# Scores formed one item ahead, a fourth buffer for the decayed r, and routing steps behind the mask products

## Chip, cores and metric

One core of a Trainium2 chip. The metric is device time in microseconds (us) of one execution; a profiled execution is shown beside the plain ones. The engines are TensorE (PE; its weight loads are listed as PEld), VectorE (DVE), ScalarE (ACT), GpSimd (POOL) and SyncE (SP), which issues most DMAs. Each engine works through its own instructions in order; semaphores hold an instruction until what it needs has been done elsewhere.

## What is computed

An RWKV-5 attention over 4 batches of 8 heads, 768 tokens and 48 dimensions, followed by a mixture of 8 experts in which each token goes to one expert; a token whose local gate is 0.5 or more takes the expert of the token before it.

```python
def _attn_ref(r, k, v, w, u):
    for t in range(S):
        kt, vt, rt = (k[:, :, t], v[:, :, t], r[:, :, t])
        cur = np.einsum('bhd,bhe->bhde', u[None] * kt, vt)
        y[:, :, t] = np.einsum('bhd,bhde->bhe', rt, state + cur)
        state = w[None, :, :, None] * state + np.einsum('bhd,bhe->bhde', kt, vt)

def _moe_ref(x, w_gate, w_local, w1, w2):
    logits = np.einsum('bsd,de->bse', x, w_gate)
    local_gate = 1.0 / (1.0 + np.exp(-np.einsum('bsd,de->bse', x, w_local).squeeze(-1)))
    for b in range(B):
        prev_e = -1
        for s in range(S):
            fresh_e = int(np.argmax(logits[b, s]))
            e = fresh_e if s == 0 or local_gate[b, s] < 0.5 else (prev_e if prev_e >= 0 else fresh_e)
            prev_e = e
            ...
            h = np.maximum(x[b, s] @ w1[e], 0.0)
            out[b, s] = p[e] * (h @ w2[e])
```

Here p is the softmax of the token's logits.

## The kernel before, in words

The kernel has two stages. The attention stage (`Attention.run`) takes the first 120 us or so, the experts (`Experts.run`) the rest. The change lies in the attention stage and in the routing steps (`Router`) that are woven into it.

**Items.** The attention is cut into M = 16 items, n = 0 to 15: 4 batches by 4 pairs of heads (HP = 4). An item is one batch and two heads, all 768 tokens, in six chunks of 128 tokens (NCH). Within a chunk the sum over earlier tokens is formed as a masked product of scores with v; what came before the chunk enters through a state S.

**The steps of one item**, with the engine that carries them and the line that the profile shows:
- `load` (SP, L199, L203, L204): three DMAs, r and k transposed (rk), k and v by token (kv), v transposed (vT). rk and vT have 4 buffers in turn, kv has 5. `load(n + 3)` stands at the head of iteration n.
- `scale` (POOL): ke (L217, k times powers of the decay up to the chunk's end), rw (L234, r times powers of the decay, in `decayed`) and pd (L221, r times k), each in two halves. ke and pd have two buffers, rw three. `scale(n + 1)` is issued in iteration n. From item 3 on the order is ke, rw, pd; for items 0 to 2 rw is formed on VectorE, in `keys`.
- `keys` (VectorE, L241): kw, k divided by powers of the decay; two buffers.
- `added` (TensorE, L253): 20 products of ke with v into T, a part of the PSUM tile mp.
- `states` (VectorE, L259): one scan over T that gives S for all chunks.
- `scores` (TensorE, L288, 24 products a call, two calls g = 0 and 1): rw with kw into one of the two PSUM tiles of `pairs`, which `banks` hands out in turn. A call returns the mask product (VectorE, L290), which multiplies the tile with the mask `kept` into am. The name `keep` stands for the second call's mask product, issued later.
- `own` (TensorE, L269, 8 products, then VectorE, L273): u times r times k, summed over the dimensions and laid out into the PSUM tile y; VectorE multiplies it with vT. There is one y tile. This is called the vT product below.
- `inside` (TensorE, L297, 24 products): adds am times v to y.
- `before` (TensorE, L310, 20 products, then ACT, L314): adds S times rw to y; ACT copies y to xT.
- `turn` (TensorE, L323, 6 transposes, then ACT, L325): turns xT to rows x; after the fourth pair of heads of a batch, a DMA on ACT's queue writes x to DRAM.
- `logits` (TensorE, L336, and ACT, L337), once a batch, and `token_logits` (TensorE, L342, and ACT, L343).

**The order of a common iteration n.** The program is written out by hand. TensorE has, in this order, turn(n-2), added(n), inside(n-1), before(n-1), scores(n) twice, own(n). VectorE has kw(n), S(n), the first mask product of n, the vT product of n, the second mask product of n. Where n is a multiple of 4, the second mask product stands before the vT product, and logits follow.

**Routing.** The first two batches (group 0, g = 8 in the code) are routed while the attention of the last two runs, one step an iteration from n = 9 on: `experts_of` (VectorE, L665 to L672), `keys` and `runs` (a transpose on TensorE, L679, then a scan on VectorE, L684), `turn_runs` (a transpose on TensorE, L689, and a copy on ACT to rn, L690), `last` (TensorE, L696), `one_hot` (VectorE, L702 to L709), `counts` (two products on TensorE, L716 and L717), `ranks` (ACT, L723, and VectorE, L724 to L735), `slots` and `columns`, `numbers`, `places` (VectorE, L783, twice), `summed` (TensorE, L790), `copied` (ACT, L796), `head` (a transpose on TensorE, L800, then VectorE, L804 to L821). After `head`, `heads()` issues two gathers of token rows on POOL's queue (L1037), which the first expert turns on TensorE (L1050). Most of these steps use parts of the tile mp, in which T lies too.

Of the kernel before, what the change touches and what calls it, by code (L numbers as in the profile page):

```python
# [11 lines left out]
F32 = mybir.dt.float32  # L12
# [8 lines left out]
P = 128  # L21
# [7 lines left out]
NCH = S // P  # L29
# [32 lines left out]
class Attention:  # L62
# [13 lines left out]
    def __init__(self, tc, st, rk_d, kv_d, vT_d, x_d, w_t, wp_d, kept, ident, lt, mp):  # L76
        self.tc, self.nc = tc, tc.nc
        nc = tc.nc
        self.rk_d, self.kv_d, self.vT_d, self.x_d = rk_d, kv_d, vT_d, x_d
        self.w_t, self.kept, self.ident, self.lt = w_t, kept, ident, lt  # L80

        self.late = st.enter_context(tc.tile_pool(name="late", bufs=1))
        self.wp = self.late.tile([P, H, 32], F32, name="wp")
        self.sel = self.late.tile([P, 2 * (E + 1)], F32, name="sel")
        self.inner = ExitStack()

        def pool(name, bufs, **kw):
            return self.inner.enter_context(tc.tile_pool(name=name, bufs=bufs, **kw))

        once = pool("once", 1)  # L90
        self.two = pool("two", 2)
        self.three = pool("three", 3)
        ps = pool("ps", 1, space=PSUM)

        self.pairs = [ps.tile([P, 2, 512], F32, name=f"pair{i}") for i in range(2)]
        self.py = pool("py", 1, space=PSUM)

        self.T = mp[:, 2 * P + 2:2 * P + 2 + (NCH - 1) * DH].rearrange("p (e c) -> p e c", c=NCH - 1)

        self.inv = pool("pinv", 1, space=PSUM).tile([P, HP, P], F32, name="inv")  # L100


        n = B * HP - 1
        self.rks, self.vTs = [None] * AHEAD, [None] * AHEAD
        for i in range(1, AHEAD + 1):
            self.rks[(n + i) % AHEAD] = once.tile([P, 2, NCH, P], F32, name=f"rk{i}")
        for i in range(1, AHEAD + 1):
            self.vTs[(n + i) % AHEAD] = once.tile([P, 2, C2, P], F32, name=f"vT{i}")
        self.kvs = [once.tile([P, 2 * VB + DP - DH], F32, name=f"kv{i}") for i in range(AHEAD + 1)]
        self.items = [dict() for _ in range(B * HP)]  # L110
        self.xTs, self.xs, self.lTs = {}, {}, {}
        for i in range(AHEAD - 1):
            self.load(i)
        nc.sync.dma_start(out=self.wp, in_=wp_d)


        self.step = once.tile([P, HP, DH, NCH - 1], F32, name="step")
        nc.vector.memset(self.step, 0.0)


        self.tab = tab = once.tile([P, HP, 2, P + 1], F32, name="tab")
        nc.vector.memset(tab[:, 0, :, 0:1], 1.0)
        nc.gpsimd.memset(tab[:, 1:, :, 0:1], 1.0)
        w = once.tile([P, HP, 2], F32, name="w")
        nc.vector.tensor_scalar(w[:, :, 0], w_t[:, :, 0], W_LO, W_HI, Alu.max, Alu.min)
        nc.vector.reciprocal(w[:, :, 1], w[:, :, 0])
        nc.vector.tensor_copy(tab[:, 0, :, 1], w[:, 0])
        nc.gpsimd.tensor_copy(tab[:, 1:, :, 1], w[:, 1:])
        n = 2
        while n <= P:  # L130
            m = min(n - 1, P + 1 - n)
            for engine, t in ((nc.vector, tab[:, :1]), (nc.gpsimd, tab[:, 1:])):
                engine.tensor_mul(t[..., n:n + m], t[..., 1:1 + m], t[..., n - 1:n].to_broadcast([P, t.shape[1], 2, m]))
            n += m

        self.first, self.newton = mp[:, :P + 1], mp[:, P + 1:2 * P + 1]
        nc.scalar.copy(self.first, tab[:, 0, 0])
        self.reciprocals(0)

        self.end = once.tile([P, HP, P + DP], F32, name="end")  # L140
        self.endT = once.tile([P, 2, HP, 2 * DH], F32, name="endT")
        self.align(26)
        self.warm(8)
        self.ends(slice(0, 1))
        self.turn_ends(slice(0, 1))
        self.warm(5)
# [61 lines left out]
    def scale(self, n):  # L208

        nc, t = self.nc, self.items[n]  # L210
        t["ke"] = self.two.tile([P, NCH, 2 * DH], F32, name="ke")
        t["pd"] = self.two.tile([P, NCH, P], F32, name="pd")
        t["rw"] = self.three.tile([P, NCH, P], F32, name="rw")
        hp = t["hp"]

        def ke(p):
            nc.gpsimd.tensor_mul(t["ke"][:, p::2], t["k"][:, p::2], spread(self.endT[:, p, hp], 1, C2))  # L217

        def pd(i):
            z = slice(i * C2, (i + 1) * C2)  # L220
            nc.gpsimd.tensor_mul(t["pd"][:, z], t["rT"][:, z], t["kT"][:, z])  # L221

        def rw(i):
            self.decayed(nc.gpsimd, n, slice(i * C2, (i + 1) * C2))


        for what in (ke, rw, pd) if n > 2 else (pd, ke):
            for i in range(2):
                what(i)

# [114 lines left out]
    def run(self, router, fetch, heads):  # L345
# [11 lines left out]
        for n in range(M + 1):  # L357
# [39 lines left out]
                continue  # L397
            if n < M:
                self.turn(n - 2, pair("tp"))
                if n == 3:  # L400
                    self.added(3)
                    self.reciprocals(3)
                self.keys(n)
                if n > 3:
                    self.added(n)
            if n == g + 2:
                router.keys(0, mp)
            if n == g + 3:
                router.last(0, mp[:, mp_end:])
            if n == g + 4:  # L410
                router.counts(0, [mp, mp[:, E * NC // 2:]])
            if n < M:
                self.states(n)
            if n > HP and n % HP == 1:
# [2 lines left out]
                self.chooser()  # L417
            if n == g + 1:
                router.experts_of(0, (0,))
            if n == g + 2:  # L420
                router.runs(0)
            if n == g + 3:
                router.one_hot(0, (0,))
            if n == g + 4:
                router.ranks(0, (0,))
            if n == g + 5:
# [10 lines left out]
            if n == M:  # L437
                self.turn(M - 2, pair("tp"))
            self.inside(n - 1)
            if n == g + 7:  # L440

                router.summed(0, 0)
                router.copied(0)
            self.before(n - 1)
            if n == 6:
                router.cast()
            if n == M:
                break
            if n == g + 7:
                router.head(pair("tb")[0])  # L450
                heads()
            self.scores(n, 0)()
            keep = self.scores(n, 1)
            if n == g + 1:
                router.experts_of(0, (1,))
            if n == g + 3:
                router.one_hot(0, (1,))
            if n == g + 5:
                router.places(0, 0)
            if n == g + 6:  # L460
                router.places(0, 1)
            if n % HP == 0:

                keep()
                self.own(n)
                self.logits(n // HP - 1, pair("lp")[0])
                if n == g + 4:
                    router.ranks(0, (1,))
            else:
                self.own(n)  # L470
                keep()
            if n == g + 2:
                router.turn_runs(0, mp[:, mp_end:])
        self.inner.close()


# [1228 lines left out]
```

## Time and profile before

| | us |
|---|---|
| plain runs, median of 4 | 388.93 (388.45 to 391.17) |
| profiled execution | 390.51 |
| its span | 388.8 |
| TensorE busy in the span | 372.9 |
| first score product of item 0 (L288) | 7.51 |
| first transposes of iteration 16 (L323, n = 16) | 110.75 |
| first transposes of expert rows (L1050) | 119.23 |
| last gathered rows written (last L1263 issue) | 382.18 |

In the order of time, an entry gives the start of a group of like instructions, the time from its start to its end, the engine, the line, the operation, what it writes and reads, the count, and in brackets how long the engine had been idle and what released it. "issue" means that the profile shows nothing the engine waited for. Over the stretch of items 5 to 15 POOL's groups come in the order ke, rw, pd. The page's slices of the span (40 slices of 9.7 us each) read, in tenths:

```profile
PE   7999999999989999999999999999999999999992
DVE  6887577688934473488657647757767758556400
POOL 8679999787222022511243212312413203112022
PEclk9999999999989999999999999999999999999998
DMA  7999998989012982650544145245156145054011
```

The first twelve slices are the attention stage. PEclk is the clock granted to TensorE; apart from the last slice, it is lower only in the twelfth, at the change from one stage to the other.

### The profile page before, as it was taken

The numbers are of one execution on the slowest core, as the hardware profiler recorded it, in microseconds if no ns is written. First come the engines' busy times: TensorE is split into PE (matmuls) and PEld (weight loads), VectorE is DVE, ScalarE is ACT, GpSimd is POOL, SyncE is SP. The second block draws the span as 40 slices with busy tenths as digits, with TensorE's granted clock in tenths as the row PEclk, the third lists the DMA queues.
The fourth block names the chain that finished last, engine by engine and source line by source line (L and its number), as shares of the span: only waits on it lengthen the run. The fifth ranks groups of instructions, "written<-read, shape, count | busy, mean of one in ns | idle before, by whom it ended". The sixth has DMA issues, their size and how long they took to land. (4 is left out here: it accounts for less than half of the span.)

```text
span 388.8 us, 9723 instructions
## 1 busy us (share of the span) xinstructions
PE 372.9 (96%) x3858; PEld 329.3 (85%) x3858; DVE 247.6 (64%) x718; ACT 107.3 (28%) x293; POOL 151.0 (39%) x212
## 2 busy tenths in 40 slices
PE   7999999999989999999999999999999999999992
PEld 6776877686767998999999999999999999999971
DVE  6887577688934473488657647757767758556400
ACT  4132222223212211222323234224224234222220
POOL 8679999787222022511243212312413203112022
PEclk9999999999989999999999999999999999999998
DMA  7999998989012982650544145245156145054011
GB/s 260 411 409 411 408 396 283 353 304 390 34 32 81 372 343 78 231 203 23 182 133 153 42 169 204 65 178 203 55 183 224 37 164 215 32 194 184 2 36 36
DMA packets 17477, 74.97 MB, mean 193 GB/s; under 512 B 2729, under 2 KB 6586, under 8 KB 14864
## 3 DMA queue, kind: packets, MB, share of 16 engines
q1 hardware_dynamic: 10048, 56.89, 38.8%
q0 software_dynamic: 3424, 9.52, 7.4%
q10 hardware_dynamic: 3952, 7.87, 5.5%
q8 instruction: 32, 0.52, 0.5%
q14 instruction: 21, 0.17, 0.1%
HBM read 64.83 MB, written 9.51 MB: 191 GB/s over the span
## 5 line engine op out<-in xcount | busy, mean ns | idle before, releaser
L1263 POOL DMA_INDIRECT out_dram<-yo,sid x27 | 26.6, 987 | 102.3 <-ACT yo L1258 78.8
L1114 PE MATMUL h<-exT,w1t 128*128 128x168 f32 (+4 forms) x240 | 54.9, 327 | 0.0
L1118 DVE TENSOR_TENSOR hT<-h,hs 128x168 f32<-128x168 f32 (+3 forms) x60 | 21.1, 351 | 46.5 <-PE h L1114 30.5
L1037 POOL DMA_INDIRECT xg<-x_d,gid x29 | 31.1, 1072 | 38.2 <-DVE sm L872 17.4
L1114 PEld LDWEIGHTS h<-exT,w1t 128*128 128x128 f32 x240 | 41.7, 190 | 0.3 <-issue 0.3
L290 DVE TENSOR_TENSOR am<-pair,kept 128x768 f32<-128x768 f32 x32 | 30.1, 952 | 15.1 <-PE pair L288 14.7
L1064 PE MATMUL h<-exT,w1t 128*128 128x192 f32 (+1 forms) x192 | 38.2, 337 | 0.0
L1183 PE MATMUL y<-factors,sums 128*128 128x192 f32 x168 | 36.8, 326 | 0.0
L1114 PE MATMUL h<-xs,ws 128*128 128x168 f32 (+4 forms) x144 | 35.2, 326 | 0.0
L1064 PEld LDWEIGHTS h<-exT,w1t 128*128 128x128 f32 x192 | 32.3, 190 | 1.4 <-issue 0.2
L221 POOL TENSOR_TENSOR pd<-rk 128x384 f32<-128x384 f32 x32 | 31.8, 1012 | 3.3 <-PE mp L253 1.3
L297 PE MATMUL y<-am,kv 128*64 128x128 f32 x384 | 29.6, 284 | 3.2 <-DVE y L273 2.4
L297 PEld LDWEIGHTS y<-am,kv 128*64 128x64 f32 x384 | 25.4, 139 | 4.5 <-DVE y L273 3.0
L1114 PEld LDWEIGHTS h<-xs,ws 128*128 128x128 f32 x144 | 25.5, 190 | 4.3 <-ACT hs L1121 1.2
L1183 PEld LDWEIGHTS y<-factors,sums 128*128 128x128 f32 x168 | 28.9, 190 | 0.0
L217 POOL TENSOR_TENSOR ke<-kv,endT 128x288 f32<-128x288 f32 x32 | 24.9, 798 | 4.3 <-DMA kv<-in_kv_dram 3.5
L234 POOL TENSOR_TENSOR rw<-rk,tab 128x384 f32<-128x384 f32 x26 | 23.6, 926 | 5.3 <-PE y L310 5.3
L314 ACT COPY xT<-y 128x768 f32<-128x768 f32 (+1 forms) x16 | 12.5, 779 | 42.6 <-PE y L310 42.6
L288 PE MATMUL pair<-rw,kw 48*64 48x128 f32 (+1 forms) x768 | 22.4, 249 | 1.3 <-ACT end L168 0.6
L1183 PE MATMUL y<-w2t,hT 128*128 128x192 f32 x96 | 23.0, 328 | 0.0
L1051 DVE COPY exT<-tp 128x384 f32<-128x384 f32 (+6 forms) x29 | 14.0, 489 | 13.8 <-PE tp L1050 13.6
L288 PEld LDWEIGHTS pair<-rw,kw 48*64 48x64 f32 x768 | 19.4, 133 | 2.7 <-issue 0.9
(279 smaller groups left out, 733.4 us busy)
## 6 DMA issues: line engine op xcount, KB each, us to landing
w1t<-in_w_dram SPq DMA_DIRECT2D x9, 1536.0 KB, 6.5
w2t<-in_w_dram SPq DMA_DIRECT2D x9, 1536.0 KB
rk<-in_rk_dram SPq DMA_DIRECT2D x15, 768.0 KB, 8.4
kv<-in_kv_dram SPq DMA_DIRECT2D x16, 584.0 KB, 8.3
vT<-in_vT_dram SPq DMA_DIRECT2D x16, 384.0 KB, 10.6
x_d<-x ACTq DMA_DIRECT2D x4, 1152.0 KB, 12.3
w1t<-in_w_dram ACTq DMA_DIRECT2D x1, 1536.0 KB
w2t<-in_w_dram ACTq DMA_DIRECT2D x1, 1536.0 KB
```

The source lines that it names most:

```text
L217: nc.gpsimd.tensor_mul(t["ke"][:, p::2], t["k"][:, p::2], spread(self.endT[:, p, hp], 1, C2))
L221: nc.gpsimd.tensor_mul(t["pd"][:, z], t["rT"][:, z], t["kT"][:, z])
L234: engine.tensor_mul(t["rw"][:, z], t["rT"][:, z], spread(pw, 1, z.stop - z.start))
L288: nc.tensor.matmul(sc[f * DP:(f + 1) * DP, h, i, x:], lhsT=t["kw"][q, c, o * DP:(o + 1) * DP], rhs=t["rw"][q, c, x:], start=True, stop=True)
L290: return lambda: nc.vector.tensor_mul(t["am"][:, g], sc, spread(self.kept[:, g:g + 3], 1, 2))
L297: nc.tensor.matmul(t["y"][p * DP:(p + 1) * DP, h, c2 * P:(c2 + 1) * P], lhsT=t["v"][:, (2 * c + h) * DH:(2 * c + h) * DH + DP], rhs=t["am" ...
L1037: self.nc.gpsimd.indirect_dma_start(out=xg[:n], out_offset=None, in_=self.x_d[:rows], in_offset=bass.IndirectOffsetOnAxis(ap=u["gid"][:n, ...
L1064: nc.tensor.matmul(h[:, :n], lhsT=u["w1"][:, m, kk, :], rhs=u["xT"][:, kk, :], start=(kk == 0), stop=(kk == DK - 1))
L1114: nc.tensor.matmul(out, lhsT=a, rhs=b, start=start and k == 0, stop=stop and k == len(terms) - 1, skip_group_check=True)
L1118: nc.vector.tensor_tensor(out, a, b, op=Alu.add)
L1183: return lambda: nc.tensor.matmul(bank[:, x * half:(x + 1) * half], lhsT=a, rhs=b, start=(j == 0 and x == 0), stop=(j == FK // 2 - 1), ski ...
L1263: self.nc.gpsimd.indirect_dma_start(out=out.rearrange("n (h d) -> (n h) d", h=2) if half else out, out_offset=bass.IndirectOffsetOnAxis(ap ...
```

## The change

rw gets a fourth buffer. `scale` orders POOL's work rw, ke, pd from item 5 on. From n = 5 on iteration n forms the scores of item n + 1 instead of those of item n, and the keys kw of item n + 2 behind the vT product; iteration 4 forms the scores of items 4 and 5 and the keys of 5 and 6; iteration 15 forms none. `router.keys` and `runs` go from the head of iteration 10 to its end, `turn_runs` from the end of 10 to the head of 11, `counts` ahead of added(12), `one_hot` becomes one step again, `places` and the second half of `experts_of` go behind the second mask product, `summed` and `copied` behind `before`, `head` and the two gathers behind own(15).

```diff
-        self.three = pool("three", 3)
+        self.four = pool("four", 4)
...
-        t["rw"] = self.three.tile([P, NCH, P], F32, name="rw")
+        t["rw"] = self.four.tile([P, NCH, P], F32, name="rw")
...
-        for what in (ke, rw, pd) if n > 2 else (pd, ke):
+        for what in (pd, ke) if n < 3 else (ke, rw, pd) if n < 5 else (rw, ke, pd):
             for i in range(2):
                 what(i)
...
             if n < M:
                 self.turn(n - 2, pair("tp"))
+                if n == g + 3:
+                    router.turn_runs(0, mp[:, mp_end:])
+                if n == g + 4:
+                    router.counts(0, [mp, mp[:, E * NC // 2:]])
                 if n == 3:
                     self.added(3)
                     self.reciprocals(3)
-                self.keys(n)
+                if n < 5:
+                    self.keys(n)
                 if n > 3:
                     self.added(n)
-            if n == g + 2:
-                router.keys(0, mp)
             if n == g + 3:
                 router.last(0, mp[:, mp_end:])
-            if n == g + 4:
-                router.counts(0, [mp, mp[:, E * NC // 2:]])
             if n < M:
                 self.states(n)
...
-            if n == g + 2:
-                router.runs(0)
             if n == g + 3:
-                router.one_hot(0, (0,))
+                router.one_hot(0)
...
             self.inside(n - 1)
-            if n == g + 7:
-
-                router.summed(0, 0)
-                router.copied(0)
             self.before(n - 1)
...
             if n == g + 7:
-                router.head(pair("tb")[0])
-                heads()
-            self.scores(n, 0)()
-            keep = self.scores(n, 1)
+
+                router.summed(0, 0)
+                router.copied(0)
+
+            ahead = n if n < 5 else n + 1
+            if ahead < M:
+                self.scores(ahead, 0)()
+                keep = self.scores(ahead, 1)
+            if n % HP == 0:
+
+                keep()
+                self.own(n)
+                self.logits(n // HP - 1, pair("lp")[0])
+                if n == 4:
+                    self.keys(5)
+                    self.scores(5, 0)()
+                    self.scores(5, 1)()
+                    self.keys(6)
+                else:
+                    self.keys(n + 2)
+                if n == g + 4:
+                    router.ranks(0, (1,))
+            else:
+                self.own(n)
+                if 4 < n < M - 2:
+                    self.keys(n + 2)
+                if ahead < M:
+                    keep()
             if n == g + 1:
                 router.experts_of(0, (1,))
-            if n == g + 3:
-                router.one_hot(0, (1,))
+            if n == g + 2:
+                router.keys(0, mp)
+                router.runs(0)
             if n == g + 5:
                 router.places(0, 0)
             if n == g + 6:
                 router.places(0, 1)
-            if n % HP == 0:
-
-                keep()
-                self.own(n)
-                self.logits(n // HP - 1, pair("lp")[0])
-                if n == g + 4:
-                    router.ranks(0, (1,))
-            else:
-                self.own(n)
-                keep()
-            if n == g + 2:
-                router.turn_runs(0, mp[:, mp_end:])
+            if n == g + 7:
+                router.head(pair("tb")[0])
+                heads()
         self.inner.close()
```

## The prediction

> **What bounds the kernel now.** I read the page's busy times first, then the order of time of TensorE alone over the attention stage, then VectorE and POOL over the same stretch, last the granted clock second by second.
>
> ```profile
> span 388.8 us, 9723 instructions
> ...
> PE 372.9 (96%) x3858; PEld 329.3 (85%) x3858; DVE 247.6 (64%) x718; ACT 107.3 (28%) x293; POOL 151.0 (39%) x212
> ```
>
> TensorE is the bound: 15.9 us of the span are free of it, and what leaves the attention stage earlier leaves the kernel earlier by as much. The expert stage isn't touched. In the attention stage the starts of L323 (`turn`) mark the iterations: 37.31 (n = 5), 43.60, 49.54, 55.99, 63.61 (n = 9), 69.90, 77.11, 83.04, 90.60, 96.90, 103.19 (n = 15), 110.75. One iteration runs without a wait, n = 9 (order of time, TensorE; start, length, line):
>
> ```profile
> 63.61 0.80 PE L323 MATMUL pair<-ident,xT 112*128 112x112 f32 x6
> 64.33 0.66 PE L253 MATMUL mp<-kv,ke 128*48 128x48 f32 x20
> 64.92 0.84 PE L342 MATMUL pair<-sel,lT 128*128 128x18 f32 x6
> 65.69 1.58 PE L297 MATMUL y<-am,kv 128*64 128x128 f32 x24
> 67.20 0.79 PE L310 MATMUL y<-rw,S 48*48 48x128 f32 x18
> ...
> 67.84 1.27 PE L288 MATMUL pair<-rw,kw 48*64 48x128 f32 x46
> 69.10 0.88 PE L269 MATMUL y<-pd,w_t 48*64 48x384 f32 x8
> ```
>
> Start to start: turn 0.72, added 0.59, token logits 0.77, inside 1.51, before 0.64, scores 1.26, own 0.80; 6.29 in all, 5.52 without token logits. Logits add 1.43 where n is 8 or 12 (62.18 to 63.61). Against that the iterations lose: n = 6 0.42, n = 7 0.93, n = 8 0.67, n = 10 1.32 (after its two routing turns of 0.21 and 0.16), n = 14 0.77, n = 15 0.99 (after 0.79 for `summed` and 0.26 for `head`). That is 5.1 us, all the change can win before the end. It has two kinds:
>
> ```profile
> 71.42 0.65 PE L297 MATMUL y<-am,kv 128*64 128x128 f32 x4
> 72.85 1.47 PE L297 MATMUL y<-am,kv 128*64 128x128 f32 x20 [0.78 <-issue]
> ...
> 97.62 0.66 PE L253 MATMUL mp<-kv,ke 128*48 128x48 f32 x20
> 98.62 1.94 PE L297 MATMUL y<-am,kv 128*64 128x128 f32 x24 [0.34 <-DVE y L273]
> ```
>
> The first is an "issue" gap, which waits for no engine; n = 7, 8 and 10 hold some 2.2 us of them (0.57, 0.31, 1.32). The second waits for VectorE: inside needs the second mask product, the last of the previous iteration, and lasts 1.87 instead of 1.51 in n = 6, 7, 8 and 14; in n = 14 it also waits for the vT product, which stands behind 1.15 of routing at 96.54.
>
> **The change, part by part.** (1) *Scores one ahead, from n = 5.* Inside(n-1) then finds its masks a whole iteration old, and waits only for the vT product, which starts 0.99 after own (69.10 to 70.09) and takes 0.97: 1.96, against own + turn + added = 2.11 on TensorE. So the waits on VectorE go: 3 x 0.36 in n = 6 to 8, 0.77 in n = 14, together -1.85. The issue gaps wait for no engine; I keep them (0), at the bound -2.2.
>
> VectorE's chain per iteration is S 0.56, mask, vT product, kw, mask at 0.87 each, 4.04 under 5.52. Its last mask ends at own + 0.99 + 2 x 0.87 + 0.96 = 3.69, and the bank it frees is wanted at 0.80 + 0.72 + 0.59 + 1.51 + 0.64 = 4.26. POOL must now give rw(n+1) within iteration n: in the rows it is busy without a break from 26 to 66 us, some 5.5 a item, and with rw first rw(7) would end near 46.9, rw(8) 52.0, rw(9) 57.3, where the scores want them near 50.0, 55.6 and 62. The fourth buffer ends POOL's waits on L310 (5.3 us in five), worth nothing: POOL waits on own for pd anyway. ke, now second, is done at 48.4 for item 7 (wanted near 52.7). SP: the rk slot's last reader becomes pd instead of kw, so its loads issue up to 1.5 us sooner (52.47 after kw at 51.46, pd done at 50.05); kw(n+2) is read at the end of iteration n, where its load has had more than an iteration for a median of 8.4 us. All this costs nothing; if a load were late, each item would lose what it is late by.
>
> (2) *Getting ahead, n = 4.* There kw(5), the scores of 5 and kw(6) stand after the logits. Nothing before them moves, so kw(5) keeps its row:
>
> ```profile
> 37.39 0.94 DVE L241 TENSOR_TENSOR kw<-rk,inv 128x768 f32<-128x768 f32 x1
> ...
> 70.09 0.97 DVE L273 TENSOR_TENSOR y<-y,vT 128x768 f32<-128x768 f32 x1
> 70.96 0.95 DVE L290 TENSOR_TENSOR am<-pair,kept 128x768 f32<-128x768 f32 x1
> ...
> 73.25 0.39 DVE L684 TENSOR_TENSOR_SCAN run<-mp,seg 12x128 f32<-12x128 f32 x1
> ```
>
> TensorE is free at 37.31 and starts the scores at 38.40: +1.09. Today this kw is hidden by turn, added, token logits, inside and before; they now stand behind it. The mask of those scores starts 0.79 later and ends at 40.15; turn(3) needs its bank, TensorE is free at 39.66: +0.55. Sum +1.64; the scores themselves (1.26) are paid back in n = 15, which has none.
>
> (3) *Routing moved.* In n = 10 `runs` now follows vT product, kw(12) and mask on VectorE, and `turn_runs` stands in n = 11 behind turn(9) on TensorE. With own(10) starting at T: the vT product starts T+0.99, then three steps of 0.87, so the scan runs from T+3.60 to 3.99, and `turn_runs` starts T+4.05. TensorE is there at T + 0.80 + 0.21 + 0.73 = 1.74. That is a new wait of 2.31. Queued behind it: added(11), last, inside, before, scores(12); S(11) and ACT's xT copy wait for those. And added(11) writes the PSUM tile that ACT's rn copy reads; accesses of that tile take turns, as here, where ACT reads other columns than the scan and starts only at the scan's end (85.83 + 0.65):
>
> ```profile
> 86.51 0.24 ACT L723 COPY ext<-mp 128x96 f32<-128x96 f32 x1 [1.93 <-DVE S L259]
> ```
>
> The rn copy starts 0.26 after `turn_runs` (76.95 to 77.21) and takes 0.17, so added waits 0.3 more. Together +2.6. `counts` finds its input an iteration old: 0. The 2.15 of `places` go behind the masks: the vT product of n = 14 comes 0.15 late and S(15) holds `summed` back 0.2 (as today, 0.34), but the 0.99 that n = 15 loses goes: -0.64.
>
> (4) *The clock in n = 11.* With (3) no product runs from own(10) to added(11): 4.56 - 0.80 = 3.76 us, but for six plus two turns. The nearest row is the end of this stage, where products rest from 110.69 to 113.04, turns apart:
>
> ```profile
> 109.86 0.83 PE L269 MATMUL y<-pd,w_t 48*64 48x384 f32 x8
> 110.75 0.79 PE L323 MATMUL pair<-ident,xT 112*128 112x112 f32 x6
> 113.04 2.83 PE L297 MATMUL y<-am,kv 128*64 128x128 f32 x24 [1.50 <-DVE y L273]
> ...
> 113.00:114.00 1.00, 0.96 (x13) 0.86 0.34 98
> 114.00:115.00 1.00, 1.00 (x11) 0.50 0.00 0
> ```
>
> The last two lines are the clock view (columns: length, TensorE busy and instructions, granted clock, DMA): 0.50 from about 113.9 to 117.1, 3.2 us at half rate, so 1.6 lost. A rest of 2.35 brought it, the issue gap of n = 10 (0.78 idle) did not; 3.76 is nearer the first. I take +1.6; bounds 0 and 1.6. [...]
>
> (5) *The end.* In n = 15 the scores are gone, `summed` and `head` follow before and own. From own(15) to the first expert turn (109.86 to 119.23) the kernel takes 9.37. Why the vT product is late there (DVE 112.02, own + 2.16 instead of 0.99) no row says; the half clock comes after it. Without both the new order would need 2.05 to inside, 1.51, 0.64, two xT copies with their hops 1.3, logits 0.9: 6.4. The two gathers then issue near own + 2.8 and 4.4 and land near 6.4, just in time. So 0 to -3.0. What surrounds the late product (own, turn, gathers) all stays, and only the rest of the products shrinks, so I take a third: -1.0.
>
> **Sum**: -1.85 + 1.64 + 2.6 - 0.64 + 1.6 - 1.0 = +2.35. The profiled execution took 390.51, 1.58 more than the median of 388.93; I add the difference to the median: **391.3**. About 0.5%, 1.94 us, is what a measurement here can tell from no change.
>
> **Rivals.** *A, the clock holds in n = 11.* [...] Against: the rest at the end was shorter. +2.35 - 1.6 = +0.75: 389.7. Chance 0.27.
> *B, not slower: the end.* Between 109.86 and 119.23 the late vT product and the half clock after it go, because products rest there 1.25 (head and turn) instead of 2.35. Price -3.0, -2.0 against my sum: 389.3 with the half clock in n = 11, 387.7 without. It decides once the vT product starts less than 1.1 after own(15). If the issue gaps also shrink by 2.2, 385.5. For it: nothing in the trace explains the lateness. Against: the median runs are faster than the profiled one and may not have it to give. Chance 0.23.
> *C, the change doesn't do what it says:* scores wait for POOL's rw in each item. Items 6 to 14 at 0.5 each, +4.5: 395.8. Against: 3 us and more of slack above. Chance 0.07.
> My forecast has 0.43, with its own range 390.3 to 393.0.
>
> Slower: 0.37 of the forecast, 0.03 of A, all of C, 0.47. Within: 0.06, 0.21 and 0.06 of B, 0.33. Faster: 0.03 of A, 0.17 of B, 0.20. The range takes in A, most of B and the half clock coming already in n = 5 (+1.6 on my sum, 392.9): 386.3 to 393.5.
>
> **What would show it.** L297 at 1.51 in n = 6 to 8 and 14; L288 after logits at n = 4 idle 1.1 behind L241; L689 idle 2.3 behind L684, the largest wait of the stage; granted clock 0.50 for about 3 us after it; L273 at own + 2.2 or + 1.0 in n = 15. I am wrong if L689 doesn't wait, or if idle time behind POOL's L234 appears ahead of L288.

## The result, and the profile after

The changed kernel took 390.03 us (median of 52 runs, 387.90 to 393.52), the kernel before, run beside it, 389.74 (78 runs, 387.95 to 393.38). The ratio is 1.0015, 95% interval 1.0000 to 1.0030: +0.6 us, not to be told from no change. A second comparison (`after_again` below) gave 1.0034 (1.0005 to 1.0064). The forecast was +2.4 us.

The profiled execution took 388.3. Its page, columns as before:

```profile
span 386.6 us, 9699 instructions
...
PE 369.3 (96%) x3858; PEld 326.9 (85%) x3858; DVE 250.6 (65%) x718; ACT 107.3 (28%) x293; POOL 150.5 (39%) x212
...
POOL 8779999849222031611333222312403213012022
PEclk9999999989999999999999999999999999999998
```

The granted clock is now low in the ninth slice (77.3 to 87 us), inside the attention stage, and no longer in the twelfth. What TensorE waited for from 27 to 120 us (engine, tile, line, releaser: sum, times, longest):

```profile
PE mp L700 <- DVE run L695: 2.1, 1, 2.1
PE pair L323 <- DVE am L290: 1.3, 2, 0.7
PE pair L288 <- DVE kw L241: 1.1, 1, 1.1
...
PE mp L253 <- issue: 0.3, 1, 0.3
```

In the kernel before this list began with 1.8 for the vT product and three issue gaps of 0.8, 0.5 and 0.4. Of what took their place the first and third row and the last were foretold, and of the second the wait in iteration 4. (Router lines stand 11 lower now: `turn_runs` is L700, `run` L695.) The two stalls at the head of the new order, in the order of time of TensorE:

```profile
38.21 1.24 PE L288 MATMUL pair<-rw,kw 48*64 48x128 f32 x48 [1.10 <-DVE kw L241]
40.06 0.80 PE L323 MATMUL pair<-ident,xT 112*128 112x112 f32 x6 [0.62 <-DVE am L290]
```

and iteration 11, which lasts from 75.54 to 85.47:

```profile
75.54 0.79 PE L323 MATMUL pair<-ident,xT 112*128 112x112 f32 x6
78.47 0.23 PE L700 MATMUL mp<-ident,run 12*128 12x12 f32 x1 [2.13 <-DVE run L695]
79.00 0.66 PE L253 MATMUL mp<-kv,ke 128*48 128x48 f32 x20 [0.30 <-issue]
79.59 0.39 PE L707 MATMUL mp<-rn,ident 128*128 128x12 f32 x2
79.91 2.36 PE L297 MATMUL y<-am,kv 128*64 128x128 f32 x24
```

L297 takes 2.36 here and 1.58 in iteration 10, because the clock falls on the way (stretch in us and its length; then busy time, with counts, of TensorE, its weight loads, VectorE, ScalarE and POOL; granted clock, DMA share, GB/s):

```profile
80.00:81.00 1.00, 1.00 (x15) 1.00 (x17) 0.88 (x4) 0.00 (x0) 1.00 (x2) 0.77 0.89 352
81.00:82.00 1.00, 1.00 (x12) 0.87 (x9) 0.86 (x4) 0.00 (x0) 0.35 (x1) 0.50 0.50 206
82.00:83.00 1.00, 1.00 (x19) 0.80 (x20) 0.03 (x1) 0.00 (x0) 0.00 (x0) 0.50 0.19 80
83.00:84.00 1.00, 1.00 (x32) 1.00 (x26) 0.00 (x0) 0.23 (x1) 0.00 (x0) 0.52 0.72 132
```

TensorE is busy in all four rows, and what the clock takes from them is 0.23 + 0.50 + 0.50 + 0.48 = 1.7 us.

Where the time came from and went is read from the starts of L323. The length of each iteration, in us, for the profile shown before, a second profile of that kernel (`before_2nd` below, from another comparison), and the changed one:

| iteration | before | before_2nd | after | after less before_2nd |
|---|---|---|---|---|
| 4 | 7.76 | 7.48 | 10.51 | +3.03, of which 1.26 are scores from iteration 15 |
| 5 | 6.29 | 6.29 | 6.20 | -0.09 |
| 6, 7, 8 | 5.94, 6.45, 7.62 | 5.78, 6.14, 7.90 | 5.33, 5.34, 6.76 | -0.45, -0.80, -1.14 |
| 9 | 6.29 | 6.29 | 6.20 | -0.09 |
| 10 | 7.21 | 6.93 | 5.65 | -1.28 |
| 11 | 5.93 | 5.84 | 9.93 | +4.09 |
| 12 | 7.56 | 7.56 | 7.15 | -0.41 |
| 13, 14 | 6.30, 6.29 | 6.29, 6.30 | 6.99, 5.33 | +0.70, -0.97 |
| 15, to own(15) | 6.67 | 6.67 | 4.58 | -2.09, of which -1.26 are the scores |
| own(15) to the expert rows' turn | 9.37 | 6.68 | 7.52 | +0.84 |

The last column sums to +1.34. Its last row compares two single executions; (5) below says what other profiles show there. Two other things weren't foretold. Iterations 6 to 8 and 10 lose 3.67. Of these 1.08 (three waits of 0.36) were counted on, and 0.09 each is lost in iterations 5 and 9 as well, which had no wait and no gap; the rest, some 2.2, are the issue gaps. Where L297 of iteration 10 stood still for 0.78 in the kernel before, it now runs in one piece (the changed kernel, then `scores_alone`, an experiment below):

```profile
71.11 1.58 PE L297 MATMUL y<-am,kv 128*64 128x128 f32 x24
...
71.70 1.58 PE L297 MATMUL y<-am,kv 128*64 128x128 f32 x24
```

And iteration 13 grew. At its end TensorE waits for a mask product (the first row is the head of iteration 14):

```profile
99.61 0.79 PE L323 MATMUL pair<-ident,xT 112*128 112x112 f32 x6 [0.71 <-DVE am L290]
100.33 0.66 PE L253 MATMUL mp<-kv,ke 128*48 128x48 f32 x20
100.81 1.55 PE L297 MATMUL y<-am,kv 128*64 128x128 f32 x24
```

L297 takes 1.55 here, with no wait before it, where it took 1.94 after a wait of 0.34 in the kernel before: the masks are an iteration old, as foretold. But the mask that L323 waits for is late. VectorE and POOL in the order of time, just before:

```profile
93.37 1.70 POOL L234 TENSOR_TENSOR rw<-rk,tab 128x384 f32<-128x384 f32 x2
93.50 0.78 DVE L741 TENSOR_SCALAR far<-pos 128x24 f32<-128x24 f32 x1
94.31 0.79 DVE L742 TENSOR_TENSOR pos<-pos,far 128x24 f32<-128x24 f32 x1
95.02 1.55 POOL L217 TENSOR_TENSOR ke<-kv,endT 128x288 f32<-128x288 f32 x2
95.02 0.82 DVE L744 COPY ext<-exc 128x8 f32<-128x8 f32 x1
95.88 0.71 DVE L745 TENSOR_SCALAR ext<-exc 128x2 f32<-128x2 f32 x1
```

Four tiny routing steps take 0.7 to 0.8 each; in the kernel before (L730 to L734) the first took 0.93 and the others 0.18, 0.17 and 0.17. They end at 94.28, 95.10, 95.84 and 96.59, and POOL's four halves (each row holds two, of 0.85 and 0.78) at 94.22, 95.07, 95.80 and 96.57. So POOL's new order, costed at nothing, became a question for the experiments.

### The profile page after: what moved, and what is told of

Same layout as the page of the kernel before. It is cut to its first block, busy times and chain, and to the rows that moved or that the text cites. A ratio compares the mean times of both kernels' runs of the same rounds, so it can differ in the third digit from the quotient of the medians.

```text
span 386.6 us, 9699 instructions
## 1 busy us (share of the span) xinstructions
PE 369.3 (96%) x3858; PEld 326.9 (85%) x3858; DVE 250.6 (65%) x718; ACT 107.3 (28%) x293; POOL 150.5 (39%) x212
## 5 line engine op out<-in xcount | busy, mean ns | idle before, releaser
L297 PE MATMUL y<-am,kv 128*64 128x128 f32 x384 | 26.6, 283 | 0.8 <-DVE y L273 0.8
L288 PE MATMUL pair<-rw,kw 48*64 48x128 f32 (+1 forms) x768 | 23.5, 251 | 2.2 <-DVE kw L241 1.1
L297 PEld LDWEIGHTS y<-am,kv 128*64 128x64 f32 x384 | 22.8, 139 | 1.3 <-DVE y L273 1.2
L288 PEld LDWEIGHTS pair<-rw,kw 48*64 48x64 f32 x768 | 20.4, 135 | 4.1 <-issue 2.4
L1062 DVE COPY exT<-tp 128x384 f32<-128x384 f32 (+6 forms) x29 | 14.0, 489 | 13.7 <-PE tp L1061 13.5
```

Of the source, the lines that this page charges most:

```text
L288: nc.tensor.matmul(sc[f * DP:(f + 1) * DP, h, i, x:], lhsT=t["kw"][q, c, o * DP:(o + 1) * DP], rhs=t["rw"][q, c, x:], start=True, stop=True)
L297: nc.tensor.matmul(t["y"][p * DP:(p + 1) * DP, h, c2 * P:(c2 + 1) * P], lhsT=t["v"][:, (2 * c + h) * DH:(2 * c + h) * DH + DP], rhs=t["am" ...
```

## Experiments

Ratios are to the kernel before on the same chip, with their 95% intervals; times are medians. The median of the kernel before lay between 386.72 and 389.74 in these comparisons, so times of different comparisons are not set side by side. Every kernel here computes the same result. The first theory was that the two new stalls and the low clock that follows them (iterations 4 and 11) give back what the new order of the scores wins.

**The changed kernel again, and its two stalls undone in turn.** `after_again` is the changed kernel.

> The changed kernel once more, to see what its profile keeps and what it draws anew. Theory 1 (the clock's phase): the wait of about 2.1 us ahead of L700 and the 1.1 ahead of L288 at n = 4 come back, the issue gaps stay away, and only the stretches of half clock move from run to run; plain runs again fall into groups by granted clock (about 0.992 near 388.3 us, 0.985 to 0.988 near 390, 0.979 near 393), ratio to before 1.000 to 1.003. Theory 2 (the scatter has nothing to do with the waits): waits and issue gaps differ from the first profile by more than 0.3 us each.

387.84 us, 1.0034 (1.0005 to 1.0064). The stall on the run is 2.1 again, the low clock lasts from 79.6 to 86.4 this time, 6.8 us instead of 3.4, and there are no issue gaps in iterations 6 to 8 and 10.

`runs_early` puts the routing keys, their scan and `turn_runs` back where the kernel before has them:

```diff
-                if n == g + 3:
-                    router.turn_runs(0, mp[:, mp_end:])
...
                     self.added(n)
+            if n == g + 2:
+                router.keys(0, mp)
...
+            if n == g + 2:
+                router.runs(0)
...
-                router.keys(0, mp)
-                router.runs(0)
+                router.turn_runs(0, mp[:, mp_end:])
```

> The changed kernel with keys, runs and turn_runs of the router back at the places of before. Theory 1 (new waits and the half clock they bring eat the gain): the 2.1 us ahead of L700 are gone, iteration 11 takes about 6 us instead of 9.9 and has full clock, and the median falls by 2.4 (wait alone) to 4.5 (with the half clock): ratio to before 0.988 to 0.995. Rival (that time is absorbed later, since the experts are bound by something else): the attention stage ends 2.4 us sooner and the median is as before, ratio 0.999 to 1.003.

388.52 us, 1.0043 (1.0014 to 1.0073): a miss. The wait moved:

```profile
PE mp L691 <- DVE key L684: 2.9, 1, 2.9
```

The change also set the second half of `experts_of`, which makes the key, behind iteration 9's mask products. Taking back one of two edits that only work together leaves the stall one link up the chain, with the low clock from 73.2 to 80.1 after it.

`keys_early` moves kw(5) ahead, right behind S(4):

```diff
+            if n == 4:
+                self.keys(5)
             if n + 1 < M:
...
-                    self.keys(5)
                     self.scores(5, 0)()
```

> The changed kernel with the keys of item 5 formed right behind the scan of item 4, where VectorE is idle for 1.5 us, instead of behind the vT product of item 4. Theory 1: the 1.1 us ahead of L288 at n = 4 are gone and the 0.6 ahead of the following L323 stay; 1.1 us faster than the changed kernel, ratio to before 0.996 to 1.000, and fewer runs with a granted clock of 0.98 if that wait brings one of the half-clock stretches. Rival (the early wait only lets loads and POOL get ahead, and a wait of the same size appears by n = 7): no difference to the changed kernel beyond 0.3 us.

387.84 us, 1.0023 (1.0006 to 1.0039). The 1.1 of L288 is gone and L323 waits 0.33 instead of 0.62, but the ratio is above the expected range: a miss. The median equals that of `after_again`; the spread is what shrank, 387.18 to 388.46 instead of 386.59 to 391.11. The wait on the run is 2.4 here, with the low clock from 78.0 to 84.9 in the profile, and all twelve runs have a mean granted clock of 0.985 to 0.990 (`after_again`: 0.977 to 0.993).

`both` has the two edits.

> Both edits together: router steps at the places of before, keys of item 5 early. Theory 1: the two gains add, 3.5 us faster than the changed kernel at equal clock and up to 6 in the median; ratio to before 0.984 to 0.992, nearly all runs with a granted clock of 0.99 or more. Rival (gains are absorbed): ratio 0.998 or more.

387.74 us, 1.0013 (0.9990 to 1.0035), a miss as well; the wait on the key is 3.0, with the low clock from 74.7 to 78.1 after it.

**What the stall in iteration 11 costs.** `before_2nd` is the kernel before, for a second profile of it.

> The kernel before, profiled a second time. Theory 1 (the first profile caught an unlucky end, which the typical run doesn't have): the vT product of item 15 starts about 1.0 after its own, there is no half clock between 105 and 120 us, own(15) to the first expert turn takes about 6.5 instead of 9.4, and the issue gaps of iterations 7, 8 and 10 (2.2 us) are at least in part elsewhere or gone. Rival (the end of before is always slow and the change wins it back): 9 us or more again with the clock at 0.5 in it. Ratio of the times 0.998 to 1.002 either way.

386.93 us, 0.9989 (0.9966 to 1.0012). Its column in the table above has 6.68 us for the end, where the first profile took 9.37, and there is no low clock in its attention stage. Issue gaps are there again in iterations 8 and 10.

`filled` lets TensorE work through the wait of iteration 11: nine products of the identity with itself into the tile that `turn` overwrites. They add nothing to the result.

```diff
-                self.turn(n - 2, pair("tp"))
+                tp = pair("tp")
+                if n == g + 3:
+                    for i in range(9):
+                        self.nc.tensor.matmul(tp[0][:, :P], lhsT=self.ident, rhs=self.ident, start=True, stop=True)
+                self.turn(n - 2, tp)
```

> The changed kernel with 9 idle products of the identity with itself ahead of turn(9) in iteration 11: they fill the wait for the scan and add nothing to the result. Theory 1 (the half clock comes from the stretch of 3.8 us without products): the wait ahead of L700 shrinks to under 0.7, the clock stays at 1.00 from 70 to 95 us, and the median is 1.6 (one stretch) to 3.3 us (two) below the changed kernel, ratio to before about 0.995 to 0.999. Rival (idle time isn't what lowers the clock, or only idle time with transposes in it): half clock around 80 us as before, ratio to before 1.003, as the changed kernel on the same footing.

386.32 us, 0.9992 (0.9962 to 1.0023). The clock in two places of its profile:

```profile
41.00:42.00 1.00, 1.00 (x8) 0.72 (x8) 1.00 (x2) 0.00 (x0) 1.00 (x2) 0.50 0.99 404
...
80.00:81.00 1.00, 1.00 (x11) 1.00 (x11) 1.00 (x2) 0.00 (x0) 1.00 (x3) 1.00 0.96 377
```

At 80 us, where the changed kernel had 0.77 and then 0.50, it is 1.00. The nine products only take the place of the wait, so what iterations 10 and 11 win, 14.4 us together instead of 15.6 in the changed kernel's profile and 17.1 in `after_again`, is the clock; that speaks for the rest of TensorE as what brings it down there. But in this execution the clock is low after the stall of iteration 4, from 40.5 to 47.4. The runs fall into two groups, seven from 385.47 to 386.32 with a mean clock of 0.994 to 0.996 and five from 388.67 to 389.90 with 0.984 to 0.988.

`mid` takes the chain apart: key and scan stand ahead of own(10), `turn_runs` behind it.

```diff
-                if n == g + 3:
-                    router.turn_runs(0, mp[:, mp_end:])
...
             else:
+                if n == g + 2:
+                    router.keys(0, mp)
+                    router.runs(0)
                 self.own(n)
...
-                router.keys(0, mp)
-                router.runs(0)
+                router.turn_runs(0, mp[:, mp_end:])
```

> The changed kernel with keys and runs of the router between the scores of item 11 and own(10), the scan ahead of the vT product, and turn_runs behind own(10). No step of the routing waits then: key is there at about 4.4 into iteration 10, the transpose stands at 4.7. Theory 1 (wait and half clock in iteration 11 eat the gain): no wait over 0.4 ahead of the router's transposes, full clock from 70 to 95 us, iteration 11 takes 5.5 to 6.0 instead of 9.9 to 11.2; 4 to 5.5 us below the changed kernel, ratio to before 0.988 to 0.994. Rival (the gain is absorbed later in the kernel): attention ends that much sooner, ratio 0.999 or more.

383.96 us, 0.9921 (0.9895 to 0.9947). The wait on the run is gone, TensorE waits 0.5 ahead of the key's transpose, the clock holds (1.00 from 75 to 85 us); one of the ten runs, 386.87 with a mean clock of 0.987, stands apart. This is 0.9 to 1.1% under the ratios of the changed kernel and bears the first theory out for iteration 11: stall and clock together cost some 4 us there, as iteration 11's +4.09 says.

`mid_early` adds the edit of `keys_early`.

> The same with the keys of item 5 early as well. Theory 1: another 1.1 us less than with the router's steps alone, ratio to before 0.985 to 0.991: faster than both kernels. Rival (absorbed): 0.999 or more.

383.71 us, 0.9906 (0.9877 to 0.9936); runs from 383.01 to 384.04.

**The change's parts alone.** `scores_alone` is the kernel before with the new order of scores and keys only (the diff's lines with `ahead`, `keys(5)`, `keys(6)`, `keys(n + 2)`).

> The kernel before with the scores one item ahead alone: keys, scores and the start in iteration 4 as in the change, POOL's order, three buffers and all routing steps as before. Theory 1 (the issue gaps and the waits for the second mask product belong to the order of before, the loss to the routing's new places): iterations 6 and 7 take 5.3 to 5.4 us, no issue gap over 0.25 in 6 to 10, the 1.1 and 0.6 of iterations 4 and 5 are there, no wait over 1 us from 65 to 95 us; ratio to before 0.990 to 0.997. Rival (the gain of the changed order needs POOL's order and the fourth buffer): TensorE waits on L234 ahead of L288, ratio 0.998 to 1.005.

384.70 us, 0.9963 (0.9938 to 0.9988): -1.4 us, with both stalls of iteration 4 still in it, and in five of the twelve runs (386.63 to 388.16, mean clock 0.986 to 0.989) what looks like the low clock. The other seven, 383.81 to 384.78 with 0.993 to 0.997, have a median 2.6 under the kernel before. Iterations 6 and 7 last 5.34 and 5.33, and the issue gaps are gone there: this part alone is enough to remove them.

`late_runs_alone` is the kernel before with only `keys`, `runs` and `turn_runs` moved.

> The kernel before with keys, runs and turn_runs of the router at the places of the change and nothing else. Theory 1: here one step less stands ahead of the scan on VectorE, so TensorE waits 1.4 to 1.8 us ahead of the transpose of run, with half clock behind it in some runs; ratio to before 1.003 to 1.009. Rival (the wait is covered, since the order of before has slack of its own): below 1.002.

391.05 us, 1.0081 (1.0059 to 1.0104): +3.1 us. Its profile is of its longest run, and in it the low clock, from 75.6 to 89.3, begins behind an issue gap in iteration 10 and before the wait on the run:

```profile
74.23 1.36 PE L297 MATMUL y<-am,kv 128*64 128x128 f32 x19 [2.46 <-issue]
...
82.55 0.28 PE L688 MATMUL mp<-ident,run 12*128 12x12 f32 x1 [0.87 <-DVE run L683]
```

So the time is in the range expected, but how much of it is the moved steps and how much the gap this run doesn't tell.

`pool_alone` is the kernel before with only POOL's part (rw first, four buffers).

> The kernel before with POOL's order (rw first from item 5) and four rw buffers alone. Theory 1: nothing on TensorE waits for it, the waits of POOL on L310 (5.3 us) go and come back as waits for own ahead of pd; ratio 0.997 to 1.003. Rival (POOL's lag causes the issue gaps): iterations 7, 8 and 10 lose 1.5 us or more less, ratio 0.992 to 0.996.

388.61 us, 1.0036 (1.0016 to 1.0055): +1.4 us from a part that was costed at nothing, and outside both expected ranges. No issue gap over 0.25 is left in iterations 6 to 10 here, nor in `first_alone` below (iteration 8 lasts 7.62 and 7.20, 7.90 in `before_2nd`), so POOL's order bears on the gaps too. VectorE and POOL at iteration 9:

```profile
65.65 3.48 DVE L667 TENSOR_TENSOR eq<-lt,mx 128x96 f32<-128x96 f32 x1
65.83 1.67 POOL L234 TENSOR_TENSOR rw<-rk,tab 128x384 f32<-128x384 f32 x2
67.47 1.55 POOL L217 TENSOR_TENSOR ke<-kv,endT 128x288 f32<-128x288 f32 x2
...
69.47 1.95 POOL L221 TENSOR_TENSOR pd<-rk 128x384 f32<-128x384 f32 x2 [0.45 <-PE y L269]
...
70.35 0.80 PE L323 MATMUL pair<-ident,xT 112*128 112x112 f32 x6 [1.05 <-DVE am L290]
70.48 0.96 DVE L671 TENSOR_TENSOR k<-t,k 128x12 f32<-128x12 f32 x1
71.38 1.95 POOL L234 TENSOR_TENSOR rw<-rk,tab 128x384 f32<-128x384 f32 x2
71.48 0.92 DVE L672 SCALAR_TENSOR_TENSOR key<-lt,k 128x12 f32<-128x12 f32 x1
```

The comparison L667 takes 3.48 and ends at 69.13, when POOL pauses (67.47 + 1.55 = 69.02). In the kernel before POOL's rw waited 0.78 for L310 in the middle of this stretch, a pause the new order no longer has, and the same steps were short:

```profile
66.32 1.22 DVE L667 TENSOR_TENSOR eq<-lt,mx 128x96 f32<-128x96 f32 x1
68.20 1.69 POOL L234 TENSOR_TENSOR rw<-rk,tab 128x384 f32<-128x384 f32 x2 [0.78 <-PE y L310]
69.75 0.17 DVE L671 TENSOR_TENSOR k<-t,k 128x12 f32<-128x12 f32 x1
69.96 0.17 DVE L672 SCALAR_TENSOR_TENSOR key<-lt,k 128x12 f32<-128x12 f32 x1
```

Behind the late comparison stands the mask that frees TensorE's bank: 1.05. So a pause of an engine that is off the path gave room to one that is on it.

`places_ahead` is `mid_early` with `places` ahead of the vT products of items 13 and 14, as before the change.

> The version with the scan ahead of the vT product of item 10 and the keys of item 5 early, with the two steps of places back ahead of the vT products of items 13 and 14. Theory 1: the vT products come about 1 us late in both, inside of iterations 14 and 15 waits 0.6 to 0.9 each; 1.2 to 1.8 us above that version, ratio to before about 0.994 to 0.996. Rival (the mask product that turn waits for is late anyway, so the order behind it is free): ratio 0.990 to 0.992.

385.16 us, 0.9942 (0.9923 to 0.9960), against 0.9906 for `mid_early` in another comparison: the new place is worth about 1.4 us. The two intervals overlap a little, but the profiles agree: iterations 14 and 15 are 1.4 longer here, and L297 waits 1.3 for the vT product, 0.3 there.

**POOL's part: which half, and is it paid in the changed kernel?** `four_alone` has only the fourth buffer, `first_alone` only the order; `after_old_pool` is the changed kernel and `mid_old_pool` is `mid_early`, each with POOL as in the kernel before:

```diff
-        t["rw"] = self.four.tile([P, NCH, P], F32, name="rw")
+        t["rw"] = self.three.tile([P, NCH, P], F32, name="rw")
...
-        for what in (pd, ke) if n < 3 else (ke, rw, pd) if n < 5 else (rw, ke, pd):
+        for what in (ke, rw, pd) if n > 2 else (pd, ke):
```

> The kernel before with only the fourth buffer of rw; POOL's order stays ke, rw, pd. Theory 1a (the buffer does it: without it POOL waits for L310 and stands idle while VectorE does its small steps): 1.002 to 1.005, an eq (L667) of 2 to 3.5 us and L671, L672 of 0.9. Theory 1b (the order does it): 0.999 to 1.001, eq 1.2 and the small ones 0.17 as in the kernel before.

389.79 us, 1.0001 (0.9973 to 1.0029).

> The kernel before with only POOL's new order rw, ke, pd from item 5 on; three buffers. Theory 1a (the buffer does it): 0.999 to 1.001, small steps as in the kernel before, POOL's waits on L310 still there ahead of rw. Theory 1b (the order does it): 1.002 to 1.005, eq (L667) of 2 to 3.5 us. Third way: rw, now first, waits for L310 and holds ke back behind it, so added (L253) waits for POOL: 1.01 or more.

390.85 us, 1.0050 (1.0020 to 1.0080). The runs lean to the order, though these two intervals overlap. The rows don't separate the two as cleanly: `four_alone` shows the long comparison too (2.80), while `first_alone` has 0.32 for it, and pays in iterations 13 and 14 instead (L767, L772 and L783 at 0.85, 1.10 and 1.43; L323 waits 1.3).

> The changed kernel with POOL's part taken back: three buffers of rw, order ke, rw, pd. It computes the same. Theory 1 (POOL's part costs about 1.4 us because it takes POOL's waits on L310 away and so puts POOL's instructions beside VectorE's small routing steps, which then last until POOL's instruction ends): ratio to the kernel before 0.997 to 1.000, some 1.0 to 1.4 us under the changed kernel; the 0.71 wait of L323 on the mask product at n = 13 is gone, the small routing steps there (L741 to L745) take 0.2 instead of 0.8. The waits at n = 4 (1.1 and 0.6) and on the run (2.1) and the half clock stay. Theory 2 (with scores formed ahead POOL's part is needed, since rw is wanted an item earlier): L288 waits for POOL, ratio 1.003 or more.

390.72 us, 1.0029 (0.9995 to 1.0063): no gain, a miss for theory 1 of these runs. The wait of 0.71 at iteration 13 is gone and L741 to L745 take 0.17 or 0.18 each, as expected. But in this profile the clock is low twice, from 41.1 to 48.0 and from 82.1 to 88.9, and the runs fall into two groups, six from 388.05 to 389.55 and six from 391.89 to 393.06. With both stalls in the kernel the scatter of the clock is larger than an effect of this size.

> The best version so far (keys and runs between the scores of item 11 and own(10), turn_runs behind own(10), kw(5) right behind S(4)) with POOL's part taken back: three buffers of rw, order ke, rw, pd. It computes the same. Theory 1: the 2.1 us in which L323 waits for mask products in four places go down to 0.7 or less, ratio 0.986 to 0.989. Theory 2 (rw is now late): waits of L288 on POOL L234, ratio 0.992 or more. No difference from the order of POOL: 0.990 to 0.992, the L323 waits as they were.

383.45 us, 0.9844 (0.9810 to 0.9878), below every expected range, beside a kernel before of 389.32; in `mid_early`'s comparison that one took 387.45. Ratio and time disagreed on the gain, so both versions were run on one chip, as `with_pool` (= `mid_early`) and `without_pool` (= `mid_old_pool`).

> The best version with POOL's part of the change (rw first, four buffers), beside the next kernel on one chip. Theory 1 (POOL's part is paid here too, as small VectorE steps that last until POOL's instruction ends and masks that come late by 2.1 to 2.4 us in sum, of which POOL's part makes some 1.5): 1.0 to 1.6 us more than the next kernel. Theory 2 (the late masks cost nothing in the end, since TensorE waits at another place instead): within 0.4 us of the next kernel.

383.82 us, 0.9896 (0.9871 to 0.9922); runs from 383.20 to 384.02.

> The same version with POOL's order and buffers as in the kernel before, beside the kernel ahead of it on one chip. Theory 1: 1.0 to 1.6 us less than that one. Theory 2: within 0.4 us of it.

382.85 us, 0.9876 (0.9851 to 0.9901); runs from 382.62 to 383.14. The two sets of runs don't overlap: 1.0 us, at the lower end of what theory 1 expected. Late masks cost `with_pool` four waits of L323, 2.1 in sum, `without_pool` one of 0.3. So POOL's part is paid with the scores ahead too, where the clock doesn't cover it, and the scores don't need it. This is the best version: 4.75 us under the kernel before on the same chip. Its iterations 10 and 11 in TensorE's order of time:

```profile
74.74 0.28 PE L691 MATMUL mp<-ident,key 128*12 128x128 f32 x1 [0.75 <-DVE S L259]
74.94 0.88 PE L269 MATMUL y<-pd,w_t 48*64 48x384 f32 x8
75.91 0.23 PE L701 MATMUL mp<-ident,run 12*128 12x12 f32 x1
76.07 0.80 PE L323 MATMUL pair<-ident,xT 112*128 112x112 f32 x6
76.79 0.65 PE L253 MATMUL mp<-kv,ke 128*48 128x48 f32 x20
```

own(10) now fills the time in which VectorE scans the run, and the 2.1 are down to 0.75.

## Why the prediction was wrong

The time on record, 391.3, is 1.3 over the measured one, but the change was forecast at +2.4 and measured at +0.6. Step by step, in us:

| step | forecast | measured |
|---|---|---|
| (1) waits on VectorE go in 6 to 8, issue gaps stay | -1.08 | -3.7 in iterations 5 to 10 of `scores_alone` against `before_2nd`, some 2.1 of it gaps |
| (1) and (3) n = 14 and the new place of `places` | -0.77 - 0.64 | about -1.4 (`places_ahead` against `mid_early`) |
| (2) two stalls at iteration 4 | +1.64 | 1.10 + 0.62 = +1.72 |
| (3) wait on the run | +2.6 | 2.13 + 0.30 = +2.43 |
| (4) low clock in iteration 11 | +1.6 | +1.7 in the profile after; up to 3.4, half of 6.8, in `after_again` |
| POOL's order and buffer | 0 | +1.4 alone, +1.0 in the best version |
| (5) the end | -1.0 | -1.85 against the first profile, +0.84 against the second, -1.0 between the means of all profiles |

**The step that failed is in (1)**: "The issue gaps wait for no engine; I keep them (0), at the bound -2.2." The other bound was the right one: with the scores ahead they went altogether, some 2.2 us of them in the table of iterations. That a gap waits for no engine was taken for a reason that the order of the program can't remove it, and that didn't follow. What the gaps are isn't settled: POOL's order bears on them as well, no run changed them by themselves, and the profile names no releaser. One trace is on record: in the DMA view a packet of the queue named "instruction" stands some 2 to 3 us ahead of the end of each listed gap (between 70 and 71 us in the kernel before, whose gap ends at 72.85). But the changed kernel has such packets as well, one between 71 and 72 us, and no gap, so they don't explain it alone.

**POOL's 0 was wrong with the opposite sign**: "The fourth buffer ends POOL's waits on L310 (5.3 us in five), worth nothing". Freeing POOL wasn't neutral here, since its waits were gaps in which VectorE's small steps ran at 0.17 to 0.3 us. With POOL busy the four steps L741 to L745 took 0.78, 0.79, 0.82 and 0.71 in the profile after, each ending 0.02 to 0.06 behind one of POOL's halves; with POOL's part taken back (`after_old_pool`) they took 0.17 or 0.18. By what POOL holds such a step up no run here shows.

With the measured terms the sum is -3.7 - 1.4 + 1.7 + 2.4 + 1.7 + 1.0 - 1.0 = +0.7 with the clock low for 3.4 us, as in the profile after, and +2.4 with 6.8, as in `after_again`; +0.6 and +1.3 were measured. The two steps above are the ones that moved the sum, by -2.2 and by +1.0 to +1.4.

**(5) came out right by luck.** Its -1.0 was "a third" of a price read from one execution. From own(15) to the expert rows' turn the six profiles whose end is that of the kernel before took 6.68 (`before_2nd`, `late_runs_alone`, `pool_alone`), 7.86 (`four_alone`, `first_alone`, with a vT product as late as in the first profile) and 9.37 (the first profile, with the low clock as well). Of the thirteen with the end of the change ten took 6.35 or 6.36, the others 6.78, 6.81 and 7.52 (the profile after), and the vT product starts 0.98 or 0.99 after own(15) in all. That is 7.5 and 6.5 in the mean. So the condition of rival B came true each time, but its price of -3.0 was that of the longest profile, and adding a difference to that profile onto the median carried the execution in. Why the vT product is late in three of the six is open.

**Right in place and size**: the stalls of (2), the wait of (3), that no L288 waits for POOL's rw in the two profiles of the changed kernel (rival C), and the fall of the clock in (4). There +1.6 was taken from the row at the end of the stage, where the clock fell after 1.50 of idle time, 2.35 with the turns; in the changed kernel it fell after 2.13 + 0.30 of idle time, 3.71 with the turns between, from the end of own(10) (74.41 + 0.88) to added(11).

The parts measured apart add up to -1.4 + 3.1 + 1.4 - 1.4 = +1.7; the whole gave +0.6 and +1.3. That is within their intervals of some 1 us each, which hold the scatter of the clock.

## What to carry to other kernels

A stall can cost more than its length: here 2.43 us of waiting in iteration 11 were followed by 3.4 us of halved clock that cost 1.7 more, and by 6.8 us of it in `after_again`. So break a chain of "transpose, scan, transpose" with work that is already there, as own(10) did (2.1 down to 0.75). A gap for which the profile names no releaser need not be a fixed cost (some 2.2 us of them went here): take it as a range, and let the sum show what it does to the verdict. A step of another engine that looks free because that engine idles may be free only because of that (POOL's part, costed at 0, took 1.0 in the best version): before filling its pauses, look at what runs in them. And take the baseline of a table like the one above from several profiles, since one stretch of unchanged code lasted from 6.68 to 9.37 us in different executions here.

## What the runs showed of the hardware

- Every stretch of halved clock in the attention stage of these profiles lasted 3.4, 6.8 or 13.7 us to within 0.1 us, that is one, two or four times 3.4: 3.4 in the first profile before, the profile after, `four_alone` and `both`; 6.8 in `after_again`, `runs_early`, `keys_early`, `filled` and twice in `after_old_pool`; 13.7 in `late_runs_alone`. In the profile after, with TensorE busy throughout, the 3.4 cost 1.7 us. After the same wait of 2.1 it was 3.4 in one execution of the changed kernel and 6.8 in the next.
- The shorter stall of iteration 4 (1.1 + 0.6 idle) was followed by the low clock in `filled` and `after_old_pool` but not in the profile of the changed kernel. An issue gap of 2.46 was followed by it in `late_runs_alone`, one of 0.78 in the first profile before was not.
- Over the 52 runs of the changed kernel, those with a mean granted clock of 0.976 to 0.980 took 391.89 to 393.52, those with 0.991 to 0.993 387.90 to 390.52. The runs of `mid_early`, `with_pool` and `without_pool`, which lack the 1.1 and the 2.1, lie within 1.1 us each.
- VectorE's small routing steps varied with POOL's order and buffers: L667 (96 elements a partition) lasted 3.48 us in `pool_alone`, 2.80 in `four_alone`, 1.22 in the kernel before and 0.32 in `first_alone`, L671 (12 elements) 0.96, 0.81, 0.17 and 0.17. The masks, keys and vT products of 768 elements lasted 0.93 to 0.97 in all of these.
